# Block-sparse attention and a dropless mixture of experts on one core: the products with V of the third chunk of keys move from the step behind the scores to the step after that

## The chip, the cores and the metric

The kernel runs on one core of one Trainium2 chip, in one launch, on float32 data. The metric is the device time of one execution in microseconds (us), the median of several runs. Next to the runs there is one profiled execution, from which all rows below come.

## The reference

Two blocks follow each other. The first is block-sparse attention (B = 4 batches, H = 8 heads, S = 768 positions, D = 64): each block of 32 queries sees its own block and both neighbours, the first and the last block, and three sampled blocks; the first and the last block of queries see all keys. The second takes the 3072 rows of 512 numbers that come out, sends each to the one of 8 experts with the largest gate logit, and applies that expert's two layers.

```
scores = where(mask, (q @ k.T) / sqrt(D), -1e9)
attn   = exp(scores - max) / (sum(exp) + 1e-9)
x      = concat over heads of (attn @ v)            # (3072, 512)
logits = x @ w_gate                                 # (3072, 8)
e      = argmax(logits);  gate = softmax(logits)[e]
out    = gate * (relu(x @ w1[e]) @ w2[e])           # rows sorted by expert, then put back
```

## The kernel before, in words

**Stages.** In the first 24 us or so the kernel loads q and k of batch 0, turns them, and makes the masks. Then come 48 attention steps up to about 278 us. After that TensorE runs the experts' layers until the end, with weights that were partly loaded during the steps.

**Steps.** The list `steps` (L1321) holds (batch, group, half): a batch has six groups, the group `GL` first and then five regular groups of 128 queries; a half is four heads, that is two pairs `pr`. So steps with an even number are half 0 of a group and those with an odd number half 1. Every step computes the scores of its own half (`scores`, L342, the matmuls at L357), which ScalarE exponentiates (L362) and VectorE masks (L368), and it multiplies the exponentials of the step before by V (`attend`, L392, the matmuls at L386).

**Three chunks of keys.** A regular group's keys come in three chunks of 128: the middle keys together with the ends (chunk 0), and two chunks that end in sampled blocks (chunks 1 and 2). Each of the two tiles `ti` of 64 queries has its own rows of V in chunks 1 and 2. V lies in the tile `around`, which has two parities of five slots: groups use the parities in turn. GpSimd gathers the sampled rows with indirect DMAs from the copy of V in memory; four of them serve one group:

```
def values_of(b, g, ti, ch):                                    # L374
    return around[:, parity(b, g), 2 * ch - 1 + ti if ch else 0, :]
def fetch_values(b, g, ti, ch):                                 # L521; ch 1 here is the third chunk
    nc.gpsimd.indirect_dma_start(
        out=around[p0:, par, 1 + ti + 2 * ch, :], ...
```

In program order GpSimd issues, for the group of steps s and s+1: the gather (ti 0, second chunk) in step s-2, (ti 1, second chunk) and (ti 0, third chunk) in step s-1, and (ti 1, third chunk) at the beginning of step s itself (L1334). Ahead of each stands a one-element copy that reads something of the step (`not_before`, L537): it holds GpSimd's queue until that was written.

**Products.** `attend` runs over chunks, then pairs, heads of a pair and tiles, so a regular step has 24 products, 8 for each chunk. A float32 product is two rows in the trace, so 48 rows. Products 17 to 24 belong to the third chunk; number 18 is the first that reads the gather (ti 1, third chunk).

**Banks.** The products of a step add up in one PSUM bank `op`, taken at the first product (`bank_of`, L377). There are two such banks. `divide` (L441) reads the finished bank on VectorE: it adds a small number to the four sums, takes reciprocals and multiplies, and with half 1 it also starts the DMA of the finished 128 rows to memory (L457). The bank is free for the next user after that.

**Logits.** When both halves of a group are divided, `turn_out` (L464) transposes the rows on TensorE (L469), ScalarE copies them (L471), and `logits` (L484) multiplies them by the gate's weights into spare columns of the bank of the step (L492), from which VectorE copies them (L496). Before the change this happens in every step of half 1, for the group that was finished one step earlier (`out_of`, L1372). When the last group of a batch has its logits, `gate` and, one step later, `gate_weights` follow.

**Order.** The schedule of all five engines is by hand (`manual_schedule`, L283 and L285): each gets its instructions in the order in which the program is written. The order inside a step is: copies that place keys, scores, transposes for the next batch (L178), `turn_out`, products, logits, division, and then the gathers of `fetch_values(*nxt[:2], 0, 0)` in steps of half 0.

Of the kernel before, what the change touches and what calls it, by code (L numbers as in the profile page):

```python
# [17 lines left out]
def kernel(  # L18
# [13 lines left out]
    B, H, S, D = q.shape  # L32
# [7 lines left out]
    E = moe_w_gate.shape[1]  # L40
# [58 lines left out]
    NG = NCH  # L99
    GL = NG - 1  # L100
# [189 lines left out]
    for n in range(2 * NPR):  # L290
        pr, which = n // 2, n % 2
# [97 lines left out]
        )  # L389
        begun.add(ti)  # L390

    def attend(units_):  # L392

        for ch in range(3):
            for b, g, pr, _, e in units_:
                for hh in range(2):
                    for ti in range(2):
                        x = 2 * ch + ti
                        product(b, g, pr, ti, hh, e[:, hh, x * D : (x + 1) * D], values_of(b, g, ti, ch), ch == 2)
# [84 lines left out]
    def logits(b, g, beside=None):  # L484
        xo = xos.pop((b, g))
        if beside is not None:
            lg = banks_of[beside][0][:, 4 * (D + 4) : 4 * (D + 4) + E]
        else:
            lg = ps_o.tile([P, E], F32, name="lgl", tag="op")[:]
        for c in range(DB):  # L490
            for j in range(2):
                nc.tensor.matmul(  # L492
                    lg[j * D : (j + 1) * D, :], lhsT=xo[:, c * P + j * D : c * P + (j + 1) * D], rhs=wg[:, c, :],
                    start=(c == 0), stop=(c == DB - 1), skip_group_check=True,
                )
        nc.vector.tensor_copy(lgn[:, b * NG + g, :], lg)  # L496
# [24 lines left out]
    def fetch_values(b, g, ti, ch):  # L521

        par = parity(b, g)
        t, p0 = tiles_of(g)[ti], 0 if ch else D
        nc.gpsimd.indirect_dma_start(  # L525
            out=around[p0:, par, 1 + ti + 2 * ch, :], out_offset=None, in_=v_d[b][:, :],
            in_offset=bass.IndirectOffsetOnAxis(ap=rows_of[: P - p0, 2 * t + ch : 2 * t + ch + 1], axis=0),
        )
# [8 lines left out]
    def not_before(at):  # L537

        nc.gpsimd.tensor_copy(paced[:], at)
# [779 lines left out]
        fill_stage(b, n // 2, n % 2, n // 2 % 2)  # L1319

    steps = [(b, g, half) for b in range(B) for g in order for half in range(2)]  # L1321
    for i, (b, g, half) in enumerate(steps):
        here = i % (2 * NG)
        prs = (2 * half, 2 * half + 1)
# [2 lines left out]
        if nxt is not None:  # L1327
            b_, g_, half_ = nxt
# [24 lines left out]
        late = here + 2 * NG * (b - B + 2)  # L1353
        for what in PARTS.get(late, ()):
            fetch_part(*what)
        if half == 1 and i + 1 < len(steps):
            not_before(mine[1][4][0:1, 0, 0:1])
            fetch_values(*steps[i + 1][:2], 0, 1)

        copy_turned = None  # L1360
        if b + 1 < B:
            if b == 0 and here < 2:
# [6 lines left out]
        if b + 2 < B and here >= 8:  # L1369
            fill_next(b + 2, here - 8)  # L1370

        out_of = steps[i - 3][:2] if i >= 3 and half == 1 else None  # L1372
        if out_of:
            turn_out(*out_of)
        if copy_turned:
            copy_turned()
        if i > 0 and before[0][1] != GL:
            attend(before)
        elif i > 0:
            for b_, g_, pr, e_all, e in before:  # L1380
                attend_last(b_, pr, e_all, e)
        if "gates" in rt:
            gate_weights()
        if out_of:
            logits(*out_of, beside=steps[i - 1])
            if out_of[1] == order[-1]:
                gate(out_of[0])
        if i > 0:
            divide(*steps[i - 1])
        early(late)  # L1390
        if half == 0 and nxt is not None:
            if i >= 2:
                fetch_ends(*nxt[:2])
                b_, g_, half_ = steps[i - 1]
                not_before(sums[0:1, b_ * NG + g_, 4 * half_ : 4 * half_ + 1])
            fetch_values(*nxt[:2], 0, 0)
        if half == 1 and nxt is not None:
# [8 lines left out]
        if i >= len(steps) - 3:  # L1406
            if i == len(steps) - 1:
                not_before(mine[1][4][0:1, 0, 0:1])
            gather(i - len(steps) + 3)
        before = mine  # L1410
    turn_x(0)
    attend(before)
    divide(*steps[-1])
    attn_by_hand.close()
    fetch(2, 1)
# [171 lines left out]
```

## Time and profile before

| what | us |
|---|---|
| runs, lowest, median, highest | 637.01, 640.93, 645.84 |
| the profiled execution's own time | 638.06 |
| its span, first to last instruction | 636.3 |
| TensorE busy in the span | 608.2 (96%) |
| VectorE, ScalarE, GpSimd busy | 315.6, 231.9, 193.8 |

The span leaves 1.8 us of the execution's time outside. A busy matmul row is not TensorE at its peak: rows overlap, and their ends are modelled. The granted TensorE clock was 0.995 of full speed over the span.

### The profile page before, as it was taken

How to read it: one execution, taken by the hardware profiler on the slowest of the kernel's cores; microseconds unless marked ns; L12 is line 12 of the kernel's file. 1: busy time of each engine (PE TensorE's matmuls, PEld its weight loads, DVE VectorE, ACT ScalarE, POOL GpSimd, SP SyncE). 2: the span in 40 equal slices, each digit the busy share in tenths (PEclk: the TensorE clock that was granted, in tenths of full speed). 3: DMA queues.
4: the chain of work that ended last, by engine and by line, in shares of the span. 5: the costliest groups of instructions: out<-in, count | busy, mean ns of one | idle time of the engine just before them, and what ended most of it. 6: DMA issues, size and time to landing. Idle time of an engine off the chain costs nothing. (4 is left out here: it accounts for less than half of the span.)

```text
span 636.3 us, 20201 instructions
## 1 busy us (share of the span) xinstructions
PE 608.2 (96%) x8326; PEld 516.0 (81%) x8326; DVE 315.6 (50%) x1025; ACT 231.9 (36%) x456; POOL 193.8 (30%) x289
## 2 busy tenths in 40 slices
PE   6899999999999899999999999999999999999994
PEld 6888999998989899997777776877878787967862
DVE  7477767675778567635852485303190118203300
ACT  5376766665667577721111011111112111111110
POOL 2157745643456445720111221011401130020110
PEclk9899999999999999999999999999999999999999
DMA  8899966995696657899999999869998999769710
GB/s 264 207 193 246 288 162 153 255 261 154 136 247 206 184 147 250 261 322 369 338 305 313 344 388 336 303 229 379 396 399 281 365 399 399 291 205 407 299 40 20
DMA packets 125061, 170.86 MB, mean 269 GB/s; under 512 B 71236, under 2 KB 71237, under 8 KB 124934
## 3 DMA queue, kind: packets, MB, share of 16 engines
q1 hardware_dynamic: 114896, 137.61, 66.3%
q0 software_dynamic: 10000, 31.59, 16.0%
q8 instruction: 75, 1.23, 0.8%
q14 instruction: 52, 0.43, 0.2%
q10 hardware_dynamic: 38, 0.00, 0.0%
HBM read 150.11 MB, written 19.33 MB: 266 GB/s over the span
## 5 line engine op out<-in xcount | busy, mean ns | idle before, releaser
L525 POOL DMA_INDIRECT around<-v_rows,rows_of x88 | 100.0, 1136 | 55.3 <-DMA around<-v_rows 21.2
L362 ACT ACTIVATE ea<-s 128x768 f32<-128x768 f32 x104 | 83.6, 811 | 83.2 <-PE s L357 56.1
L1119 DVE STREAM_TRANSPOSE around<-xg 32x128 f32<-32x128 f32 x192 | 58.1, 303 | 86.9 <-DMA xg<-x_rows,gB 81.9
L1138 PEld LDWEIGHTS hp<-around,room 128*128 128x128 f32 x832 | 94.7, 192 | 3.9 <-issue 3.2
L1138 PE MATMUL hp<-around,room 128*128 128x128 f32 x832 | 96.8, 276 | 0.6 <-issue 0.3
L386 PE MATMUL op<-around,ea 128*64 128x65 f32 x2112 | 85.5, 224 | 8.8 <-DMA around<-v_rows,rows_of 5.1
L386 PEld LDWEIGHTS op<-around,ea 128*64 128x64 f32 x2112 | 75.4, 137 | 15.5 <-DMA around<-v_rows,rows_of 6.1
L368 DVE TENSOR_TENSOR ea<-ea,mask 128x768 f32<-128x768 f32 x80 | 74.6, 955 | 14.7 <-ACT ea L362 10.1
L1152 PE MATMUL zp<-room,kr 128*128 128x512 f32 x176 | 77.6, 594 | 0.0
L1145 ACT ACTIVATE kr<-hp 128x512 f32<-128x512 f32 x36 | 21.4, 597 | 116.0 <-PE hp L1138 98.3
L1172 POOL DMA_INDIRECT out_dram<-kr,sB x14 | 14.1, 1008 | 160.2 <-ACT kr L1162 97.9
L1152 PEld LDWEIGHTS zp<-room,kr 128*128 128x128 f32 x176 | 32.6, 190 | 37.2 <-issue 37.2
L357 PE MATMUL s<-other,kr 64*128 64x128 f32 x704 | 48.1, 272 | 0.3 <-issue 0.3
L357 PE MATMUL s<-room,kr 64*128 64x128 f32 x704 | 47.9, 272 | 0.2 <-issue 0.2
L1138 PEld LDWEIGHTS hp<-around,other 128*128 128x128 f32 x384 | 43.8, 192 | 2.3 <-issue 2.3
L1138 PE MATMUL hp<-around,other 128*128 128x128 f32 x384 | 44.3, 275 | 0.0
L357 PEld LDWEIGHTS s<-other,kr 64*128 64x128 f32 x704 | 43.7, 188 | 0.6 <-issue 0.6
L357 PEld LDWEIGHTS s<-room,kr 64*128 64x128 f32 x704 | 43.7, 188 | 0.0
L1250 DVE STREAM_TRANSPOSE ea<-ea 32x128 f32<-32x128 f32 x84 | 21.7, 285 | 30.9 <-DMA ea<-x_rows,gB 30.2
L1162 ACT ACTIVATE kr<-zp,xg 128x512 f32<-128x512 f32 x12 | 8.2, 687 | 74.9 <-PE zp L1152 74.9
L1152 PE MATMUL zp<-other,kr 128*128 128x512 f32 x80 | 35.3, 593 | 0.0
L1119 DVE STREAM_TRANSPOSE around<-kr 32x128 f32<-32x128 f32 x48 | 14.5, 302 | 36.3 <-PE hp L1138 34.9
(369 smaller groups left out, 831.2 us busy)
## 6 DMA issues: line engine op xcount, KB each, us to landing
room<-in_moe_w_dram SPq DMA_DIRECT2D x30, 2048.0 KB
other<-in_moe_w_dram SPq DMA_DIRECT2D x16, 2048.0 KB
room<-in_moe_w_dram SPq DMA_DIRECT2D x16, 512.0 KB
x_rows<-xb SPq DMA_DIRECT2D x20, 256.0 KB
room<-in_k_dram SPq DMA_DIRECT2D x24, 192.0 KB
room<-in_q_dram SPq DMA_DIRECT2D x24, 192.0 KB
v_rows<-room SPq DMA_DIRECT2D x12, 260.0 KB
v_rows<-other SPq DMA_DIRECT2D x12, 260.0 KB
```

The source lines that it names most:

```text
L357: nc.tensor.matmul(s[:, hh, a : a + P], lhsT=keys(r), rhs=moving, start=True, stop=True)
L362: nc.scalar.activation(e, s[:, :, : 6 * D], AF.Exp, scale=scale)
L368: nc.vector.tensor_tensor(e, e, m[:, None, :].to_broadcast([P, 2, 6 * D]), op=ALU.mult)
L386: nc.tensor.matmul(op[ti * D : (ti + 1) * D, pr % 2, hh, : D + 1], lhsT=e, rhs=values[:, (2 * pr + hh) * VW : (2 * pr + hh + 1) * VW], sta ...
L525: nc.gpsimd.indirect_dma_start(out=around[p0:, par, 1 + ti + 2 * ch, :], out_offset=None, in_=v_d[b][:, :], in_offset=bass.IndirectOffsetO ...
L1119: nc.vector.transpose(xT[d, :, t], xg[t, :DM].rearrange("p (c q) -> p c q", c=DB)[:, :, d])
L1138: nc.tensor.matmul(hp[:, m, :], lhsT=st[i]["w1"][:, c, fb * P : (fb + 1) * P], rhs=st[i]["xT"][:, c, :], start=(c == 0), stop=(c == DB - 1),)
L1145: nc.scalar.activation(hT[:, g * (FB // 2) : (g + 1) * (FB // 2), :], hp[:], AF.Relu)
L1152: nc.tensor.matmul(zp[:], lhsT=st[i]["hT"][:, fb, :], rhs=st[i]["w2"][:, fb, :], start=(fb == 0), stop=(fb == FB - 1),)
L1162: nc.scalar.activation(zo, zp[:], AF.Copy, scale=of_i)
L1172: ins = nc.gpsimd.indirect_dma_start(out=to[:, :], out_offset=bass.IndirectOffsetOnAxis(ap=at, axis=0), in_=rows, in_offset=None, bounds_c ...
L1250: nc.vector.transpose(xT_u[d, :, j * P + tq * 32 : j * P + (tq + 1) * 32], xg_u[t, j, :DM].rearrange("p (c q) -> p c q", c=DB)[:, :, d],)
```

## The change

In a regular group the products of the third chunk no longer run in the step behind the scores but in the step after that, ahead of the first two chunks of the next half. A step n counts as split (`in_two`) when its group is regular, it isn't the last step of its batch, and it isn't one of the last four: that is so for 33 of the 48 steps. A split step's bank is closed one step later, so its division, the output rows and the logits of its group go a step later too: `turn_out` and `logits` now stand in steps of half 0 (three steps behind the group's half 1, two for the last group but one; the last group's logits stay behind the steps). In steps with logits these are written beside the closed bank, and this bank is divided behind the logits; in the others the closed bank is divided right behind the third chunk. The gather (ti 0, third chunk) in steps of half 1 is issued behind the third chunk's products, since it overwrites what they read; and the copy that holds back the gather (ti 0, second chunk) in steps of half 0 reads the sums of the bank closed in that step.

```
-    def attend(units_):
-        for ch in range(3):
+    def attend(units_, chunks):
+        for ch in chunks:
...
-            lg = banks_of[beside][0][:, 4 * (D + 4) : 4 * (D + 4) + E]
+            lg = beside[:, 4 * (D + 4) : 4 * (D + 4) + E]
...
+    def in_two(n):
+        return steps[n][1] != GL and n % (2 * NG) != 2 * NG - 1 and n < len(steps) - 4
+    out_at = {}
+    for n in range(1, len(steps) - 2, 2):
+        out_at[n + (3 if n < len(steps) - 4 else 2)] = steps[n][:2]
...
-        if half == 1 and i + 1 < len(steps):
-            not_before(mine[1][4][0:1, 0, 0:1])
-            fetch_values(*steps[i + 1][:2], 0, 1)
...
-        out_of = steps[i - 3][:2] if i >= 3 and half == 1 else None
+        units_of[i] = mine
+        out_of = out_at.get(i)
         if out_of:
             turn_out(*out_of)
...
-        if i > 0 and before[0][1] != GL:
-            attend(before)
...
+        if i > 1 and in_two(i - 2):
+            attend(units_of[i - 2], (2,))
+            closed.append(i - 2)
+            spare = banks_of[steps[i - 2]][0]
+            if not out_of:
+                divide(*steps[i - 2])
+        if half == 1 and i + 1 < len(steps):
+            not_before(mine[1][4][0:1, 0, 0:1])
+            fetch_values(*steps[i + 1][:2], 0, 1)
...
+                attend(units_of[i - 1], (0, 1) if in_two(i - 1) else (0, 1, 2))
+            if not in_two(i - 1):
+                closed.append(i - 1)
...
-            logits(*out_of, beside=steps[i - 1])
+            logits(*out_of, beside=spare)
...
-        if i > 0:
-            divide(*steps[i - 1])
+        for n in closed:
+            if steps[n] in banks_of:
+                divide(*steps[n])
...
-                b_, g_, half_ = steps[i - 1]
+                b_, g_, half_ = steps[closed[0]]
                 not_before(sums[0:1, b_ * NG + g_, 4 * half_ : 4 * half_ + 1])
```

TensorE's order in two consecutive steps of batch 0, a step of half 0 and one of half 1, in the kernel before. `op` with its number is one bank's tile, `s` the scores, `tp` the transposes for the next batch, `xr` those of finished rows; xN counts products or transposes.

```order
L178 MATMUL tp_914<-ident_58,room_75 128x64 x12
L386 MATMUL op_930<-around_78,ea_77 64x65 x24
L357 MATMUL s_995<-room_75,xk_79 128x128 x2
L357 MATMUL s_995<-room_75,kr_80 128x128 x8
L357 MATMUL s_996<-room_75,xk_79 128x128 x2
L357 MATMUL s_996<-room_75,kr_80 128x128 x8
L178 MATMUL tp_1023<-ident_58,room_75 128x64 x12
L469 MATMUL xr_1038<-ident_58,xb_850 128x64 x8
L386 MATMUL op_1050<-around_78,ea_77 64x65 x24
L492 MATMUL op_1050<-wg_63,xo_1047 64x8 x8
```

The same engine in two consecutive steps of the changed kernel, one of half 1 and one of half 0.

```order
L178 MATMUL tp_1008<-ident_58,room_75 128x64 x12
L386 MATMUL op_916<-around_78,ea_77 64x65 x8
L386 MATMUL op_1039<-around_78,ea_77 64x65 x16
L357 MATMUL s_1095<-room_75,xk_79 128x128 x2
L357 MATMUL s_1095<-room_75,kr_80 128x128 x8
L357 MATMUL s_1096<-room_75,xk_79 128x128 x2
L357 MATMUL s_1096<-room_75,kr_80 128x128 x8
L178 MATMUL tp_1121<-ident_58,room_75 128x64 x12
L469 MATMUL xr_1136<-ident_58,xb_945 128x64 x8
L386 MATMUL op_1039<-around_78,ea_77 64x65 x8
L386 MATMUL op_1156<-around_78,ea_77 64x65 x16
L492 MATMUL op_1039<-wg_63,xo_1145 64x8 x8
```

A step still has 24 products, but 8 of them close the bank opened in the step before (`op_1039` has 16 in one step and 8 in the next), and `xr` and the logits stand in the step of half 0.

VectorE's order at the end of a step with logits and the beginning of what follows, in the kernel before. `lgn` are the copied logits, `sums`, `r` and `xb` the three operations of a division, `ea` the exponentials that are masked, `kr` and `xk` placed keys.

```order
L570 COPY kr_80<-room_75 128x4x64
L368 TENSOR_TENSOR ea_77<-ea_77,mask_81 128x768 x2
L496 COPY lgn_64<-op_813 128x8
L445 TENSOR_SCALAR sums_86<-op_813 128x4
L447 RECIPROCAL r_848<-sums_86 128x4
L451 TENSOR_TENSOR xb_850<-op_813,r_848 128x256
L545 COPY around_78<-room_75 64x520
L552 COPY xk_79<-room_75 128x4x64
```

The same in the changed kernel.

```order
L570 COPY kr_80<-room_75 128x4x64
L368 TENSOR_TENSOR ea_77<-ea_77,mask_81 128x768 x2
L496 COPY lgn_64<-op_802 128x8
L445 TENSOR_SCALAR sums_86<-op_802 128x4
L447 RECIPROCAL r_943<-sums_86 128x4
L451 TENSOR_TENSOR xb_945<-op_802,r_943 128x256
L562 TENSOR_LOAD from_k_85
```

The operations of VectorE are the same; logits and division now stand together in the steps of half 0 (no copy to `around` follows there), and `op_802` is the bank that was opened a step earlier than the one that the step's last products go to.

## Rows read from the trace of the kernel before

**Rows 1.** The page's busy time by engine (busy us, share of the span, instructions), and the table by stretch: start and end, length, busy us of each engine with its instructions, granted clock, DMA share and GB/s.

```profile
PE 608.2 (96%) x8326; PEld 516.0 (81%) x8326; DVE 315.6 (50%) x1025; ACT 231.9 (36%) x456; POOL 193.8 (30%) x289
...
45.00:280.00 235.00, 224.48 (x5369) 214.25 (x5367) 160.84 (x484) 154.62 (x309) 127.24 (x196) 1.00 0.80 214
280.00:636.00 356.00, 346.96 (x2276) 267.45 (x2275) 126.62 (x459) 52.78 (x99) 52.25 (x53) 1.00 0.85 311
```

**Rows 2.** Who TensorE waited for from 45 to 280 us: us in total, times, longest.

```profile
PE op L386 <- DMA around<-v_rows,rows_of: 4.7, 6, 1.0
PE s L349 <- issue: 2.6, 5, 0.9
PE op L386 <- issue: 2.3, 6, 0.5
PE s L357 <- issue: 0.3, 1, 0.3
```

**Rows 3.** TensorE in order of time (start, length, engine, line, what, rows merged, and in brackets the idle time before it and what ended it), in two steps of half 1: the first without a stop among its products, the second with one; and the beginnings of the step behind each.

```profile
105.78 1.62 PE L386 MATMUL op<-around,ea 128*64 128x65 f32 x48
107.24 0.59 PE L492 MATMUL op<-wg,xo 128*64 128x8 f32 x16
107.76 0.49 PE L357 MATMUL s<-other,xk 64*128 64x128 f32 x4
...
114.81 0.42 PE L469 MATMUL xr<-ident,xb 64*128 64x64 f32 x8
115.16 1.47 PE L386 MATMUL op<-around,ea 128*64 128x65 f32 x34
117.59 0.62 PE L386 MATMUL op<-around,ea 128*64 128x65 f32 x13 [0.97 <-DMA around<-v_rows,rows_of]
118.62 0.49 PE L357 MATMUL s<-other,xk 64*128 64x128 f32 x4
120.96 0.54 PE L178 MATMUL tp<-ident,room 64*128 64x64 f32 x12
121.42 1.62 PE L386 MATMUL op<-around,ea 128*64 128x65 f32 x48
122.97 0.49 PE L357 MATMUL s<-other,xk 64*128 64x128 f32 x4
```

**Rows 4.** The other places among the products of regular steps at which TensorE stood still for a gather, or for "issue" at the same position; first the whole of one more such step.

```profile
135.92 1.27 PE L386 MATMUL op<-around,ea 128*64 128x65 f32 x34
137.59 0.62 PE L386 MATMUL op<-around,ea 128*64 128x65 f32 x13 [0.41 <-DMA around<-v_rows,rows_of]
138.62 0.49 PE L357 MATMUL s<-other,xk 64*128 64x128 f32 x4
...
54.73 0.62 PE L386 MATMUL op<-around,ea 128*64 128x65 f32 x13 [1.04 <-DMA around<-v_rows,rows_of]
64.79 0.62 PE L386 MATMUL op<-around,ea 128*64 128x65 f32 x13 [0.36 <-issue]
182.66 0.62 PE L386 MATMUL op<-around,ea 128*64 128x65 f32 x13 [0.90 <-DMA around<-v_rows,rows_of]
212.47 0.62 PE L386 MATMUL op<-around,ea 128*64 128x65 f32 x13 [0.73 <-DMA around<-v_rows,rows_of]
274.94 0.62 PE L386 MATMUL op<-around,ea 128*64 128x65 f32 x13 [0.67 <-DMA around<-v_rows,rows_of]
```

**Rows 5.** GpSimd in order of time from 106 to 119 us: the gathers, in the order (ti 1, second chunk), (ti 0, third chunk), (ti 1, third chunk) of the group whose products of half 0 start at 115.16, then one (ti 0, second chunk) and so on for the next group.

```profile
106.24 0.94 POOL L525 DMA_INDIRECT around<-v_rows,rows_of  x1 [0.16 <-issue]
108.21 0.98 POOL L525 DMA_INDIRECT around<-v_rows,rows_of  x1 [0.54 <-PE op L492]
110.52 1.70 POOL L525 DMA_INDIRECT around<-v_rows,rows_of  x1 [0.48 <-issue]
112.68 0.18 POOL L539 COPY paced<-sums 1x1 f32<-1x1 f32 x1 [0.46 <-DVE sums L445]
113.40 0.94 POOL L525 DMA_INDIRECT around<-v_rows,rows_of  x1 [0.54 <-issue]
```

**Rows 6.** VectorE in order of time in the same steps: the two masks of the step, then logits and division.

```profile
114.69 1.97 DVE L368 TENSOR_TENSOR ea<-ea,mask 128x768 f32<-128x768 f32 x2
119.19 0.17 DVE L496 COPY lgn<-op 128x8 f32<-128x8 f32 x1 [2.53 <-PE op L492]
119.28 0.15 DVE L445 TENSOR_SCALAR sums<-op 128x4 f32<-128x4 f32 x1
119.46 0.18 DVE L447 RECIPROCAL r<-sums 128x4 f32<-128x4 f32 x1
119.67 0.42 DVE L451 TENSOR_TENSOR xb<-op,r 128x256 f32<-128x256 f32 x1
```

**Rows 7.** TensorE at the stops among products of steps of half 0.

```profile
176.09 1.30 PE L386 MATMUL op<-around,ea 128*64 128x65 f32 x26 [0.34 <-issue]
197.81 0.71 PE L386 MATMUL op<-around,ea 128*64 128x65 f32 x17 [0.49 <-issue]
241.18 1.13 PE L386 MATMUL op<-around,ea 128*64 128x65 f32 x30 [0.35 <-issue]
250.68 1.01 PE L386 MATMUL op<-around,ea 128*64 128x65 f32 x26 [0.34 <-issue]
260.13 0.99 PE L386 MATMUL op<-around,ea 128*64 128x65 f32 x26 [0.36 <-issue]
```

More of the change, by code (lines that the diff above doesn't have):

```diff
@@ L1321 @@
     steps = [(b, g, half) for b in range(B) for g in order for half in range(2)]
+    units_of = {}
+    def in_two(n):
[3 more added lines that the diff above has]
+        out_at[n + (3 if n < len(steps) - 4 else 2)] = steps[n][:2]
     for i, (b, g, half) in enumerate(steps):
@@ L1376 @@
             copy_turned()
-        if i > 0 and before[0][1] != GL:
-            attend(before)
-        elif i > 0:
-            for b_, g_, pr, e_all, e in before:
-                attend_last(b_, pr, e_all, e)
+        closed = []
+        spare = None
+        if i > 1 and in_two(i - 2):
[7 more added lines that the diff above has]
+            fetch_values(*steps[i + 1][:2], 0, 1)
+        if i > 0:
+            if steps[i - 1][1] == GL:
+                for b_, g_, pr, e_all, e in units_of[i - 1]:
+                    attend_last(b_, pr, e_all, e)
+            else:
+                attend(units_of[i - 1], (0, 1) if in_two(i - 1) else (0, 1, 2))
+            if not in_two(i - 1):
+                closed.append(i - 1)
+                spare = spare if spare is not None else banks_of[steps[i - 1]][0]
         if "gates" in rt:
@@ L1409 @@
             gather(i - len(steps) + 3)
-        before = mine
     turn_x(0)
-    attend(before)
+    attend(units_of[i], range(3))
     divide(*steps[-1])
```

## The prediction

> **What bounds the kernel now.** I read the busy time by engine first, then the table by stretch, then who TensorE waited for, and last the order of time on TensorE, GpSimd and VectorE around those waits. In the first [rows 1] the reader sees TensorE busy for 608.2 of 636.3 us, so all its idle time is 28.1 us, and no order of the work can win more than that unless busy time shrinks. The table by stretch puts 235 − 224.5 = 10.5 us of it in the steps from 45 to 280 us, where the change acts, and 9 us into the experts' stretch, which has little more than its end. VectorE (160.8 of 235), ScalarE (154.6) and GpSimd (127.2) have room. So the steps are bound by TensorE, and the change can pay only through TensorE's stops.
>
> The list of TensorE's waits [rows 2] names them: 4.7 us for gathered rows of V, six times, never over 1.0; 2.6 us at the scores of group GL; 2.3 us of "issue" among the products. The order of time [rows 3, 4] shows where a gather stops it: each time behind 34 rows of a step of half 1, that is behind 17 products, in front of number 18. That is the first that reads (ti 1, third chunk), the gather issued last, in the step in which the scores are made. The "issue" of 0.36 us at 64.79 sits at the same place and I count it as the same wait. The change gives exactly this read one more step.
>
> **What a stop costs.** The idle time is less than the loss, because rows overlap. A step without a stop goes from its first product to the next scores in 107.76 − 105.78 = 1.98 us; with a stop of 0.97 it takes 118.62 − 115.16 = 3.46 [rows 3]. The loss is 1.48, so 0.51 more than is shown idle. At 135.92 it is 138.62 − 135.92 − 1.98 = 0.72 for an idle 0.41 [rows 4], so 0.31 more. The Trainium skill, Perfetto Trace Analysis, section Identifying the Most-Contended Engine, says that busy time of matmuls is no good measure of headroom, since they are pipelined; the trace agrees, with 1.48 us lost where 0.97 is idle. By idle time alone the gain would be 4.4 us.
>
> **The sum.** Six stops lie in steps that the change touches: 0.97 [rows 3], 0.41, 1.04, 0.36, 0.90 and 0.73 [rows 4], together 4.41 us. With 0.51 for the first and 0.31 for each of the other five the loss is 4.41 + 0.51 + 1.55 = 6.5 us. The stop of 0.67 at 274.94 [rows 4] stays: its half is one of the last four, which aren't split.
>
> **Is the gather in time a step later?** The gather for the stop at 117.59 begins at 110.52 and leaves GpSimd at 112.22 [rows 5]; TensorE goes on at 117.59, so the rows landed about 5.4 us behind. Without the stop TensorE would have wanted them at 115.16 + 1.47 = 116.6. In the changed order product 18's work comes ahead of the other products of the next step, where products now start at 121.42 [rows 3], less the 1.5 us that the stop cost: 119.9. So there are 119.9 − 112.2 = 7.7 us for a landing of 5.4.
>
> **What is late next.** The second chunk's gather (ti 1) leaves GpSimd at 106.24 + 0.94 = 107.2 [rows 5]. It is read behind 16 of the 24 products in the changed step (8 of the old half, then the first chunk), and `turn_out`, 0.34 us (115.16 − 114.81) [rows 3], no longer stands ahead: about 115.16 − 0.34 + 16 × (1.46 ÷ 24) = 115.8, with 107.24 − 105.78 = 1.46 for 24 products. That leaves 8.6 us for 5.4. The moved gather (ti 0, third chunk) waits for the third chunk's products of the same step, but already waits for the step's last mask: the masks end at 116.66 [rows 6], and those products would end near 115.16 − 0.34 + 0.5 = 115.3 [rows 3], so nothing is added. The gather that goes by the sums now waits for logits first in steps of half 0: 0.52 us of logits, `turn_out` 0.34 and a copy of 0.17 [rows 3, 6] make about 1 us, against 13 us from its issue at 113.40 [rows 5] to its read three steps on. I cost all three at nothing; the cover is the margin of 3 us or more, and if it went, a stop like those above would come back.
>
> **The banks.** There are two, and now each is open over two steps. A bank closed in a step with logits must be divided before the first two chunks of the next step begin. From the end of logits to the end of the division goes 120.09 − 118.62 = 1.5 us [rows 3, 6]. TensorE meanwhile has scores and transposes (121.42 − 118.62 = 2.8) and 8 products (0.5) [rows 3], 3.3 us in all. The margin is 1.8 us, so I cost it at nothing. Products, transposes and logits stay the same in number. No row shows a step's products go from one bank to the other: the dearest reading is the 0.09 us by which 24 products take longer ahead of scores (1.55, from 121.42 to 122.97) than ahead of logits (1.46) [rows 3], 33 × 0.09 = 3 us; the other end is the stops in steps of half 0 [rows 7], 1.88 us idle and 3.4 with 0.31 more for each, which fall away if they are waits after all. I take zero, since products within one run follow each other without a gap.
>
> Output rows and their logits go out one step later. The first routing of tokens now follows the gate in the same step; VectorE has 74 us idle over 235 [rows 1], and TensorE waits for none of it. SyncE's queue gets the output rows later, behind the same neighbours; I cost that at nothing.
>
> So the profiled execution, whose time is its span and 1.8 us around it, goes from 638.06 to 631.6. The median of the runs is 640.93, 2.9 us above it. If that difference is more of the same stops it goes too; if not it stays. I take half of it, and so predict 633.0.
>
> **Rivals.** (a) The gain is half: TensorE runs ahead by what it wins, the bus stays as busy (DMA share 0.80 [rows 1]), and gathers of the second chunk, or the banks, stop it instead in some steps. For it: TensorE and gathers follow each other closely. Against: no stop before product 17 in any half 1 of this trace. 638.06 − 3.2 + 2.9 = 637.7.
>
> (b) The stop isn't the gather's landing at all, so the order changes nothing: 640.9. What speaks for it is that 5.4 us is long for a gather. Against: the stops stand at one product in all seven cases [rows 3, 4], and only half 1, which reads the rows first, has them. The Trainium skill, DMA: Bandwidth & Descriptors, section Anatomy of one DMA — SWDGE (gpsimd) path, gives about 2.0 us plus bytes ÷ 436e3; for 128 rows of 520 floats I estimate 2.6 us by that page, and by it no gather here would have been late. The trace's 5.4 us is the measured one, on a bus that others share.
>
> (c) Slower: in steps with logits the division behind them frees the bank too late, and the first product into it waits in the next step. It decides when VectorE's division ends more than 3.3 us behind the logits, where 1.5 is seen. At 2.6 us of extra lateness each of some 18 such steps would lose 0.8 us, 14 us in all: 638.06 − 6.5 + 14.4 = 646. For it: VectorE also has masks and key copies in that order. Against: the masks end at 116.66 and VectorE then sat idle for 2.53 us before the logits [rows 6].
>
> (d) More: the stops of half 0 [rows 7] were waits too and go as well: 631.6 − 3.4 = 628.2. Against: these stand behind 17 to 31 rows, not at one product, and half 1 of a group reads rows that half 0 has read before.
>
> **How the numbers follow.** I give the forecast 0.54, (a) 0.20, (b) 0.06, (c) 0.09, (d) 0.11. The forecast's own range is 630 to 636, from the unknown costs above and the 2.9 us between execution and median. The range over cases goes from 627.0, which leaves out the better part of (d), to 642.0, which leaves out most of (c): some 15 in 100 outside. A measurement of this kernel can tell about 2% from no change, 12.8 us. Faster by over 2% is below 628.1: half of (d), 0.06 rounded up. Slower is above 653.7: the worst of (c), 0.03. The rest, 0.91, is within.
>
> **What would show it.** In the changed kernel TensorE's waits for gathers should fall from six to at most one or two, none behind the first chunk's products; products of a split step should take 1.5 us from first to next operation, in two banks; busy time of TensorE from 45 us to the end of the steps should stay near 224 us, and the steps should end about 6 us sooner, with the experts' stretch as long as before. It is wrong if stops appear at the first product into the second bank (banks), behind 16 products of a step (second chunk), or if the same six losses stand in front of the third chunk a step later; and if the steps end sooner but the experts' stretch grows by as much.

## The result and the profile after

The changed kernel takes 645.17 us (median of 20 runs, 641.57 to 654.45) where the kernel before takes 640.35 (20 runs on the same chip): a ratio of 1.0081, 95% interval 1.0059 to 1.0103. Forecast were 633.0 and a gain of 6.5 us; what came is a loss of 4.8 us, outside the range. Two repeats, the second on a faster chip, gave 1.0069 (1.0042 to 1.0095) and 1.0074 (1.0041 to 1.0106): the loss is small and steady.

The profiled execution took 641.82 us with a span of 640.1, against 638.06 and 636.3 before. Busy time and the table by stretch, to be held against [rows 1] (the last stretch here ends with the span):

```profile
PE 614.4 (96%) x8326; PEld 521.6 (81%) x8326; DVE 316.6 (49%) x1025; ACT 231.4 (36%) x456; POOL 201.6 (31%) x289
...
45.00:280.00 235.00, 222.63 (x5308) 211.92 (x5304) 159.29 (x474) 152.50 (x305) 131.08 (x194) 0.99 0.79 209
280.00:640.10 360.10, 350.48 (x2337) 270.57 (x2335) 127.85 (x463) 53.45 (x100) 54.19 (x55) 1.00 0.85 309
```

TensorE is busy for 222.6 of 235 us where it was 224.5: its idle time has grown by 1.9 us in the very stretch in which 4.4 should have gone. Who it waited for from 45 to 280 us, against [rows 2]:

```profile
PE op L386 <- issue: 3.3, 10, 1.1
PE tp L178 <- DMA room<-in_k_dram: 1.6, 1, 1.6
PE s L349 <- issue: 1.3, 3, 0.5
PE op L492 <- ACT xo L471: 1.0, 4, 0.3
...
PE tp L178 <- ACT ea L362: 0.8, 1, 0.8
PE op L386 <- DMA around<-v_rows,rows_of: 0.8, 1, 0.8
```

This is the first reading to make. The waits for gathered rows went from six (4.7 us) to one (0.8), and that one stands in the halves that are not split. So the mechanism of the change works. But three kinds of wait are new: loads of K, the copy of the rows for the logits (`xo`), and ScalarE's exponentials in front of transposes. The waits called "issue", which have no named releaser, grew from 2.3 to 3.3 us among the products (1.1 of it is one stop in step 46) and fell from 2.6 to 1.3 us in the scores of group GL.

A pair of split steps in order of time, against [rows 3] and [rows 4]: a step of half 1 and the step of half 0 with logits behind it.

```profile
112.84 0.49 PE L357 MATMUL s<-other,xk 64*128 64x128 f32 x4
...
115.64 1.62 PE L386 MATMUL op<-around,ea 128*64 128x65 f32 x48
117.19 0.49 PE L357 MATMUL s<-other,xk 64*128 64x128 f32 x4
...
120.43 1.68 PE L386 MATMUL op<-around,ea 128*64 128x65 f32 x48
...
122.58 0.49 PE L357 MATMUL s<-other,xk 64*128 64x128 f32 x4
```

24 products in two banks take 117.19 − 115.64 = 1.55 us, as before in one: the change of bank costs nothing. The pair takes 4.35 + 5.39 = 9.74 us, where the pair that ends in the stop of [rows 3] took 118.62 − 107.76 = 10.86. So where a stop goes and nothing takes its place, a pair wins a microsecond.

Where then does the time go? Three marks divide the steps in both traces. Step 5 begins (its scores) at 49.37 before and 47.84 after, step 45 at 261.44 and 260.60, and the experts' first transposes, in the kernel before, at

```profile
275.96 0.66 PE L1127 MATMUL tp<-ident,xg 128*128 128x128 f32 x4
```

and at 279.60 after. So steps 5 to 44 take 212.07 us before and 212.76 after, although the gathers' stops are gone (in a second pair of profiles on another chip it is 210.01 and 213.29, so one profile is good to some 2 us here); the last three take 14.52 and 19.00, of which 8 products that have moved into them explain 0.5. The experts' stretch is as long as before (360.3 and 360.5 us from that mark to the end). One loss is an expected gain that never came, the other is 4 us at the end of the steps.

The second is plain to see, in TensorE, ScalarE and GpSimd in order of time in step 46:

```profile
266.22 0.49 PE L357 MATMUL s<-other,xk 64*128 64x128 f32 x4
...
269.34 0.38 PE L469 MATMUL xr<-ident,xb 64*128 64x64 f32 x5 [0.31 <-issue]
...
271.55 2.13 PE L386 MATMUL op<-around,ea 128*64 128x65 f32 x42 [1.07 <-issue]
...
270.14 0.81 ACT L362 ACTIVATE ea<-s 128x768 f32<-128x768 f32 x1 [4.60 <-PE xr L469]
...
265.81 0.98 POOL L525 DMA_INDIRECT around<-v_rows,rows_of  x1 [0.55 <-issue]
267.10 0.95 POOL L1056 DMA_INDIRECT xg<-x_rows,gA  x1 [0.30 <-issue]
268.36 0.95 POOL L525 DMA_INDIRECT around<-v_rows,rows_of  x1 [0.30 <-issue]
269.61 0.95 POOL L1056 DMA_INDIRECT xg<-x_rows,gA  x1 [0.30 <-issue]
```

The step takes 8.26 us, from 266.22 to 274.48, where 4.01 was the time before (without logits, which add 0.9). TensorE trickles and ScalarE begins its first exponential 2.5 us late, both without a releaser that fits. Behind it the granted clock falls, to 0.57 over 4 us, most of it at the lower of its two levels, 1.2 GHz; before that stretch TensorE had been busy for 2.23 of 4 us. The table by stretch, with columns as in [rows 1] (the granted clock is the last but two):

```profile
268.00:272.00 4.00, 2.23 (x42) 1.84 (x40) 0.96 (x1) 1.08 (x2) 1.95 (x3) 1.00 0.83 319
272.00:276.00 4.00, 4.00 (x70) 3.98 (x67) 1.79 (x5) 1.02 (x2) 0.00 (x0) 0.57 0.51 198
```

These two losses are what the experiments take apart.

### The profile page after: what moved, and what is told of

Read it like the earlier page. It is cut to its first block, busy times and chain, and to the rows that moved or that the text cites. A ratio compares the mean times of both kernels' runs of the same rounds, so it can differ in the third digit from the quotient of the medians.

```text
span 640.1 us, 20199 instructions
## 1 busy us (share of the span) xinstructions
PE 614.4 (96%) x8326; PEld 521.6 (81%) x8326; DVE 316.6 (49%) x1025; ACT 231.4 (36%) x456; POOL 201.6 (31%) x289
## 5 line engine op out<-in xcount | busy, mean ns | idle before, releaser
L525 POOL DMA_INDIRECT around<-v_rows,rows_of x88 | 102.5, 1165 | 53.8 <-DMA around<-v_rows 22.0
L386 PE MATMUL op<-around,ea 128*64 128x65 f32 x2112 | 83.6, 225 | 5.1 <-issue 3.3
```

The source lines that it names most:

```text
L386: nc.tensor.matmul(op[ti * D : (ti + 1) * D, pr % 2, hh, : D + 1], lhsT=e, rhs=values[:, (2 * pr + hh) * VW : (2 * pr + hh + 1) * VW], sta ...
L525: nc.gpsimd.indirect_dma_start(out=around[p0:, par, 1 + ti + 2 * ch, :], out_offset=None, in_=v_d[b][:, :], in_offset=bass.IndirectOffsetO ...
```

## The experiments

The runs come in five groups: that of part 1, that of part 2, two of part 3, and that of part 4. Each group has its own chip and runs of the kernel before on it. The chips are not alike: the kernel before took 639.9 and 638.6 us in the first two groups (and 640.35 with the result above), and 630.1, 628.4 and 629.0 in the last three. So ratios are compared, and traces, where it can be done, with traces of the same kind of chip.

**1. The two halves of the change, each alone.** The changed kernel once more, with nothing edited, and the kernel before:

> The changed kernel once more, for a second profile. Time about 645 us, ratio to the kernel before 1.006 to 1.010. Theory A (the logits moved to the steps of half 0 cost time there): steps of half 0 that have logits and transposes take 5.3 to 5.5 us again, where 5.1 would be their sum, TensorE waits for the copied rows xo in several of them, and the stop of 4 us in the last but one step need not come back. Theory B (the end of the steps): the last but one step takes over 8 us again, where 4.0 is its sum, and the granted clock falls behind it.

> The kernel before once more, for a second profile: 635 to 647 us; four to seven stops for gathers behind 34 rows, each 0.4 to 1.0 us; steps of half 0 of 4.35 us where there is no stop, and no step near 8 us among the last four.

Logits and rows out moved to half 0, no product split:

```diff
 def in_two(n):
-    return steps[n][1] != GL and n % (2 * NG) != 2 * NG - 1 and n < len(steps) - 4
+    return False
```

> No step is split: the third chunk stays where it was before, but output rows are turned and logits made in steps of half 0, as in the changed kernel. Theory A: slower than before by 5 to 10 us (645 to 650), since it has the cost and not the gain; the stops for gathers behind 34 rows come back, four to seven of them. Theory B, if the third chunk or its gather is what makes the end late: as before, 640.

Products split, logits kept in half 1 (a step later again):

```diff
-    out_at[n + (3 if n < len(steps) - 4 else 2)] = steps[n][:2]
+    late_by = {1: 3, 2 * NG - 3: 3, 2 * NG - 1: 2}.get(n % (2 * NG), 4)
+    out_at[n + (late_by if n < len(steps) - 5 else 3 if n == len(steps) - 5 else 2)] = steps[n][:2]
```

> Steps are split as in the changed kernel, but the rows of most groups are turned and their logits made one step later still, in steps of half 1 as before (for the group GL and the ones at a batch's end in steps of half 0). Theory A: the gain of some 6 us comes out: 633 to 636. Theory B, or a cost in the split itself: 643 to 647, like the changed kernel.

Measured, as ratios to the kernel before: 1.0069 (1.0042 to 1.0095) for the repeat, 1.0023 (0.9991 to 1.0055) for the logits alone, 1.0035 (1.0014 to 1.0056) for the split alone. Step 46 took 8.84 us in the repeat, 7.84 with the split alone, 5.74 with the logits alone, 4.07 in the kernel before. The split alone costs a little, the logits alone can't be told from no change, neither pays, and the split alone has no wait at all for gathered rows from 45 to 280 us.

**2. The stop in step 46.** First the last six halves left whole, so that steps 44 to 47 issue what they issue before; then the same with the split alone; then SyncE's two loads of step 46 moved to 47; then the gathers of x one step later:

```diff
-    return steps[n][1] != GL and n % (2 * NG) != 2 * NG - 1 and n < len(steps) - 4
+    return steps[n][1] != GL and n % (2 * NG) != 2 * NG - 1 and n < len(steps) - 6
...
-    out_at[n + (3 if n < len(steps) - 4 else 2)] = steps[n][:2]
+    out_at[n + (3 if n < len(steps) - 6 else 2)] = steps[n][:2]
```

> The changed kernel, but the last six halves (instead of four) stay whole and the logits of the last three groups stay where the kernel before has them, so that steps 44 to 47 issue what they issue before. The changed kernel's step 46 takes 8.3 to 8.8 us from scores to scores where about 4.9 is its work, and the clock is halved for 3.4 us behind it. Theory B (that stop is most of the loss): step 46 is back at 4.0 to 4.3 us, the granted clock stays at full there, and the time is 3 to 4 us under the changed kernel, 640.3 to 641.5, within 0.2% of the kernel before. Theory A (the loss is spread over the steps of half 0 with logits, through ScalarE): the time stays within 1 us of the changed kernel, 643.5 to 645, and the steps before 42 are as in the changed kernel. Rival C (the stop belongs to whatever step comes last but one, or follows the last split step): a stop of 3 us or more shows up in step 44 to 47 all the same.

> The split of the products alone, with logits in steps of half 1, and with the last steps as in the kernel before. With the end of the changed kernel it took 641.4 us, 1.5 over the kernel before, of which the stop in step 46 (7.8 us where 4.9 is its work) was about 3. Theory B: it takes 638 to 638.7 us, 0.2 to 0.3% faster than the kernel before, since the split wins about 1.5 us in a batch's regular stretch and pays some of it back at the batch's start. If the split wins nothing even so (the stops at gathers had cover, the prediction's rival b), it takes 640 us or more. The prediction's own sum would have it at 633 to 635, since all six stops are gone.

```diff
-    PARTS |= ... | {n: [(1, 1, 2 * n - 44), (1, 1, 2 * n - 43)] for n in (22, 23)}
+    PARTS |= ... | {23: [(1, 1, part) for part in range(4)]}
```

> The changed kernel with the two quarter loads of expert 1's first weights that SyncE issues in step 46 moved behind, to step 47, where two others stand already. In the changed kernel SyncE issues them at 267.1 us, behind output rows that it waited for, and TensorE and ScalarE stop between 268.6 and 271.6. If these 512 KB on the queues are the cause of the stop, step 46 falls from 8.3 us to about 5, with no half clock behind it. If they are not, step 46 stays at 7.5 to 9 us.

```diff
-        if i >= len(steps) - 3:
+        if i >= len(steps) - 2:
             if i == len(steps) - 1:
+                gather(1)
                 not_before(mine[1][4][0:1, 0, 0:1])
-            gather(i - len(steps) + 3)
+            gather(2 * (i - len(steps) + 2))
```

> The changed kernel with the gathers of rows of x for experts 0 and 1 one step later each (46 and 47 instead of 45 and 46). GpSimd issues them at 267.1 and 269.6 us in the changed kernel, around the stop in step 46. If they are its cause, step 46 falls from 8.3 us to about 5; the transposes of expert 0's rows behind step 47 may then wait a little. If they are not, step 46 stays at 7.5 to 9 us.

In none of the four did step 46 come back to its work: it took 6.74, 6.78, 7.20 and 7.40 us (the last two are one run each). The first is telling: its steps 45 to 47 issue what the kernel before issues, and 2.7 us are lost in step 46 all the same; the ratio stayed at 1.0068 (1.0040 to 1.0096). The split alone with plain end came out at 0.9995 (0.9956 to 1.0034), where 0.997 or 0.998 was expected. TensorE in that kernel, step 46, products:

```profile
266.80 1.26 PE L386 MATMUL op<-around,ea 128*64 128x65 f32 x22
268.43 0.35 PE L386 MATMUL op<-around,ea 128*64 128x65 f32 x5 [0.36 <-issue]
269.16 0.38 PE L386 MATMUL op<-around,ea 128*64 128x65 f32 x5 [0.38 <-issue]
...
270.65 0.57 PE L386 MATMUL op<-around,ea 128*64 128x65 f32 x11 [0.37 <-issue]
```

No product here waits for a semaphore, and still they come in spurts of 5 rows, 0.74 us apart. So the order of the last steps and the weight loads are excluded. The gathers of x are not: in the last run they stand one step later in the program, but GpSimd, which was ahead, started them at 268.58 and 269.83 us, still in step 46 (267.10 and 269.61 in the changed kernel). What all of these share with the changed kernel is that GpSimd's last gathers follow each other without a pause; that gave theory C.

**3. Theory C: gathers in a row.** The gathers of x held back behind masks, on the split alone with plain end and on the changed kernel:

```diff
-        if i >= len(steps) - 3:
-            if i == len(steps) - 1:
-                not_before(mine[1][4][0:1, 0, 0:1])
-            gather(i - len(steps) + 3)
+        if i >= len(steps) - 2:
+            not_before(mine[half][4][0:1, 0, 0:1])
+            for row in range(half, 2 * half + 1):
+                gather(row)
```

> Split of the products alone, plain end, and the gathers of rows of x for experts 0 and 1 held back: the first until the first mask of step 46, the second (with the third) until the last mask of step 47. Theory C: it is GpSimd's gathers, issued one behind the other, that stop the issue of TensorE and ScalarE. In every kernel with a long step 46 three or four gathers start within 2.6 to 4.3 us of each other and the stop begins 0.6 us behind the start of the third; in the kernel before masks on VectorE held the second and third back (1.71 and 1.40 us instead of 0.95) and nothing stopped. By C step 46 falls from 6.8 us to 4.0 to 4.6, and the time from 638.5 to 635.5 to 636.5, which is 0.3 to 0.5% under the kernel before. If something else stops step 46, it stays at 6 us or more and the time at 638 to 639. A wait of up to 1 us in front of expert 0's transposes may take a part away.

> The changed kernel and nothing else than that holding back of the gathers for experts 0 and 1. Theory C: step 46 falls from 8.3 to 8.8 us to about 5, the half clock behind it is gone, and the time goes from 644 to 640 to 641. If the stop isn't the gathers', 643 to 645.

The first of these with one more gather moved, out of the rows of group GL:

```diff
+            if g == GL and i > 2:
+                fetch_values(*steps[i + 1][:2], 0, 0)
...
+                if g != GL:
                     not_before(sums[0:1, b_ * NG + g_, 4 * half_ : 4 * half_ + 1])
-            fetch_values(*nxt[:2], 0, 0)
+            if g != GL or i < 2:
+                fetch_values(*nxt[:2], 0, 0)
```

> As the split alone with held-back gathers, and in the second step of each batch but the first, the gather that started 1.1 to 1.5 us into the 96 rows of group GL's scores goes behind that step's mask. Over ten profiles those rows take 1.56 us where no gather starts between 0.6 us ahead of them and 1.25 us into them, and 2.4 to 2.9 us where one does. Theory C: in steps 13 and 25 they fall from 2.7 to 2.8 us to 1.56, in step 37 they stay near 1.6, and the time is 2 to 3 us under its sister without this edit, 633 to 634. If rows of GL are slow for another reason (clock, banks), they stay at 2.7 us and the times are the same. If the later gather is read too early, a stop of TensorE for it shows up two steps on.

And the kernel before with three gathers put in a row at four places:

```diff
             fetch_values(*steps[i + 1][:2], 0, 1)
+            if i in (17, 19, 29, 31):
+                fetch_values(*steps[i + 1][:2], 1, 0)
+                fetch_values(*steps[i + 1][:2], 1, 1)
```

> The kernel before; only in steps 17, 19, 29 and 31 the three gathers that otherwise go apart (by waits for keys, mask and keys) follow each other behind the mask of that step. Theory C: TensorE stops for 0.4 us or more without a named releaser in most of these four steps or the ones behind them, beginning about 0.6 us behind the start of the third gather, 3 us or more in all over the same steps of the kernel before when the stops for gathered rows are set aside. If the row of gathers is harmless, such stops stay at the 0 to 0.4 us that these steps show in the kernel before.

Step 46 fell to 3.99, 4.64 and 3.98 us, as C had it. But the times did not follow: 1.0028 (0.9992 to 1.0064), 1.0099 (1.0064 to 1.0134) and 0.9950 (0.9916 to 0.9984); and the crowded kernel had two unnamed stops (0.51 and 0.45 us), both at rows of GL, none near its rows of gathers. This chip was of the faster kind, so kernels with and without the holding back were run side by side on one more chip:

> The changed kernel once more, on one chip with its paced sister. Theory C (gathers issued in a row stop TensorE and ScalarE): step 46 takes 8 us or more here while the sister's takes 5 or less. If the chip decides it, both are long or both are short.

> The changed kernel with the gathers for experts 0 and 1 held back. Theory C: step 46 at about 5 us, and 2 to 4 us less time than the changed kernel on the same chip. If only the chip decided: step 46 as long as its sister's, and the same time.

> The split alone, logits in half 1, plain end, gathers as they were. On one chip it was 0.9995 of the kernel before with step 46 at 6.8 us. Theory C: 0.997 to 1.003, step 46 at 6 us or more.

> The same with the last gathers held back and one gather of each batch's second step behind its mask: 0.995 of the kernel before on one chip (interval 0.992 to 0.998). Theory C: 0.992 to 0.998 again, 2 to 4 us under its unpaced sister, step 46 at about 4 us, and rows of GL in steps 13 and 25 at 1.6 to 2.2 us. If that was the chip's doing, it is the same as its sister.

Ratios: 1.0074 (1.0041 to 1.0106), 1.0141 (1.0095 to 1.0187), 1.0056 (1.0021 to 1.0091) and 1.0024 (0.9996 to 1.0052). The changed kernel on this chip, nothing held back, GpSimd and then TensorE in step 46:

```profile
266.01 0.98 POOL L525 DMA_INDIRECT around<-v_rows,rows_of  x1 [0.54 <-issue]
267.30 0.95 POOL L1056 DMA_INDIRECT xg<-x_rows,gA  x1 [0.30 <-issue]
268.55 0.95 POOL L525 DMA_INDIRECT around<-v_rows,rows_of  x1 [0.30 <-issue]
269.81 0.95 POOL L1056 DMA_INDIRECT xg<-x_rows,gA  x1 [0.30 <-issue]
...
265.26 0.49 PE L357 MATMUL s<-other,xk 64*128 64x128 f32 x4
...
269.90 0.49 PE L357 MATMUL s<-other,xk 64*128 64x128 f32 x4
```

The same four gathers, 1.25 us apart, and the step takes 4.64 us without a stop. Gathers in a row are not enough for the stop: it comes and goes with the chip. Whether they are needed for it stays open, since no kernel with held-back gathers ran on a chip of the first kind. And holding them back makes the changed kernel slower (by about 4 us on this chip): TensorE then waits 2.8 us for rows of V in step 45, and 2.6 us for expert 1's rows of x behind the steps, where it waited for none. So the times with held-back gathers say little about theory C. That the version with 0.9950 beats the kernel before did not hold on a second chip.

What is left is the more useful fact: the changed kernel loses 0.7% here too, without the stop. Its waits from 45 to 262 us on this chip:

```profile
PE tp L178 <- DMA room<-in_k_dram: 4.6, 3, 2.5
PE s L357 <- issue: 1.7, 2, 0.9
```

**4. Theory D: the gate holds SyncE's queue.** The transposes of K for the next batch read loads that SyncE issues two steps ahead. Here is SyncE from step 26 on, in the kernel before (first trace):

```profile
167.13 0.37 SPq L517 DMA_DIRECT2D x_rows<-gw  x1
...
170.85 3.21 SPq L161 DMA_DIRECT2D other<-in_v_dram  x4
174.16 1.80 SPq L140 DMA_DIRECT2D room<-in_k_dram  x2
```

and in the changed kernel (the run on the faster chip), with TensorE at step 30's transposes:

```profile
171.46 1.17 SPq L161 DMA_DIRECT2D other<-in_v_dram  x2
175.72 0.37 SPq L517 DMA_DIRECT2D x_rows<-gw  x1
...
178.92 2.97 SPq L140 DMA_DIRECT2D room<-in_k_dram  x2
...
187.26 0.59 PE L178 MATMUL tp<-ident,room 64*128 64x64 f32 x12 [2.48 <-DMA room<-in_k_dram]
```

The four writes of gate weights (`gate_weights`, L517 and L519) need the logits of the batch's last group, and these come a step later now. So the writes stand behind two of the four loads of V shown, instead of ahead of all four; SyncE's queue, which goes in order, stands still from 172.63 to 175.72, and the K load behind it starts late. TensorE's stop in step 30 is in all three traces of kernels with the late gate on the faster chips (2.27, 2.35 and 2.48 us).

In the first trace of the changed kernel the writes are as late: they begin at 173.30 and the K load at 176.48, where the kernel before issued it at 174.16 for a step that came 2.6 us later. But there the load doesn't stop TensorE. The stop at step 30's transposes is short and ended with an exponential of ScalarE:

```profile
184.40 0.59 PE L178 MATMUL tp<-ident,room 64*128 64x64 f32 x12 [0.84 <-ACT ea L362]
```

Of the other five traces with the late gate on the first chips one has a stop for K there, of 1.26 us.

Taking the late writes alone away:

```diff
+        def write():
+            nc.sync.dma_start(x_d[first : first + GL * P, DM:].rearrange("(c p) w -> p c w", p=P), gw[:, :GL])
+            for p, n, row in pieces(GL):
+                nc.sync.dma_start(x_d[b * S + row : b * S + row + n, DM:], gw[p : p + n, GL, :])
...
+            later.append(write)
...
+        while writes:
+            writes.pop(0)()
         units_of[i] = mine
...
-            gate_weights()
+            gate_weights(writes)
```

The loop over `writes` stands in the next step, behind its load of K and so behind the loads of V of the step before.

> The changed kernel, but SyncE's four writes of gate weights go behind the loads of V and K of the next step instead of ahead of them. In the changed kernel SyncE waits for the gate until 173.3 us and issues step 30's K load at 176.5 us (174.2 in the kernel before, whose step 30 comes 2.6 us later). Theory D (the later gate holds SyncE's queue, and the K load behind it stops TensorE): the K load comes 2 us or more earlier against its step, the stop in step 30 goes, and the time is 1.003 to 1.005 of the kernel before instead of 1.007 to 1.008. Rival E (loads are bound by the bus, whatever stands ahead of them in the queue): waits for K stay at 1.5 to 4.6 us in steps 45 to 262 us of the trace, and the ratio stays at 1.006 to 1.009. The stop of step 8 (1.5 us), ahead of which no gate is written, stays in both.

> The kernel before once more, for its trace on the same chip. By the traces so far TensorE waits 3 to 6 us for gathered rows between 45 and 262 us, not at all for K, and step 46 takes 4.0 us.

Measured: 0.9992 (0.9969 to 1.0015). No loss can be told, which is more than D expected. SyncE and the same transposes in this kernel:

```profile
173.56 1.43 SPq L140 DMA_DIRECT2D room<-in_k_dram  x2
175.09 0.65 SPq L519 DMA_DIRECT2D x_rows<-gw  x1
...
183.10 0.54 PE L178 MATMUL tp<-ident,room 64*128 64x64 f32 x12
```

The load has 183.10 − 173.56 = 9.5 us and TensorE doesn't wait; step 30 takes 5.02 us instead of 7.72. Rival E, that the bus sets the loads whatever the order, is out for this stop. It holds in part for step 8, where no gate is written: there a wait of 0.8 us is left.

But the stop is a part of the loss only: 2.7 us of step 30, where the fall of the ratio is worth some 5 us. The split alone, whose gate is not late, has its K load in time on the very chip on which the changed kernel has that stop:

```profile
169.89 1.51 SPq L140 DMA_DIRECT2D room<-in_k_dram  x2
...
178.62 0.54 PE L178 MATMUL tp<-ident,room 64*128 64x64 f32 x12
```

Its ratio there was 1.0056 (1.0021 to 1.0091) all the same, where the changed kernel's was 1.0074. So on that chip the late gate is not needed for a loss. The mended kernel was not run beside the changed one, and what else lies between 1.007 and 0.999 no run shows.

The mended kernel's waits from 45 to 262 us:

```profile
PE s L357 <- issue: 4.5, 4, 2.3
PE op L386 <- DMA around<-v_rows,rows_of: 1.5, 1, 1.5
PE s L349 <- issue: 1.4, 1, 1.4
PE tp L178 <- DMA room<-in_k_dram: 0.8, 1, 0.8
```

and the longest of the kernel before on the same chip, up to 275 us:

```profile
PE op L386 <- DMA around<-v_rows,rows_of: 6.0, 8, 1.5
```

So with the queue mended one of the gathers' eight stops is left (1.5 of 6.0 us, in a half that isn't split), and other stops stand in their place. From 45 us to the end of the steps all stops together come to 9.7 us in the mended kernel, to 12.3 in the changed one of part 3 and to 6.6 in the kernel before. By these traces the mended kernel would still be slower than the one before; its profiled execution took 630.32 us, over its median of 628.70, and that of the kernel before 626.09, under its median of 628.95. So they show that new stops use up the gain, and not why the medians are equal.

## Why the prediction was wrong

**The gathers.** Right. Six stops fell to one, in the halves that stay whole, as said; no stop behind 16 products of a step, none at a new bank, 1.55 us for a step's products. Rivals (b) and (c) are out; that the 646 of (c) lies near the 645.17 measured is chance, since no product waited for a bank.

**The step that failed** is that the 6.5 us were taken as won, and all that TensorE runs into in the gathers' place was costed at nothing. "The steps should end about 6 us sooner"; on the chip of the result they ended 279.60 − 275.96 = 3.6 us later. Steps 5 to 44 took as long as before, with new stops at transposes (1.6 and 0.8 us) and logits (1.0 us), and step 46 took 8.26 us instead of 4.01. What stops step 46 is open.

One of these zeros has a cause that an edit shows, on the faster chips: "SyncE's queue gets the output rows later, behind the same neighbours; I cost that at nothing." Output rows are not all that hangs on the logits. The gate of a batch does too, and its four writes go through the same queue, ahead of loads of K that TensorE wants two steps on. The prediction said that "the first routing of tokens now follows the gate in the same step", looked at VectorE for it, and never looked at SyncE's order. Moving the writes took step 30 from 7.72 to 5.02 us. The ratio went from 1.007 to 0.999, some 5 us, but on different chips, and the rest of that is not placed. On the chip of the result TensorE did not stop for the late load.

**What is late next.** The prediction asked this of gathers and banks only. TensorE arrives at step 8 at 62.30 instead of 65.81 and wants its K 3.3 us sooner; SyncE issues the load at 56.70 instead of 57.47, 0.8 us sooner. The difference is the new stop there:

```profile
66.41 0.59 PE L178 MATMUL tp<-ident,room 64*128 64x64 f32 x12 [1.60 <-DMA room<-in_k_dram]
```

Loads that had 10.7 us before (57.47 to 68.15) have 8.1 now, and take 9.7. This is rival (a), which had the right idea (TensorE runs ahead into the next transfer) with half the price and the wrong transfers: it named the second chunk and the banks. In the mended kernel nothing of the gain is left, so the price is all of it, not half; how much of that is transfers isn't shown, since the largest part of its stops (4.5 us, in front of scores) has no named releaser.

**The logits in half 0** were given no cost. On the first chip their step takes 5.39 us where the kernel before has 5.02 for the same work in half 1, and TensorE waits 1.0 us in four places for `xo`; on the faster kind of chip it is 5.02 again. Alone, this part gave 1.0023 with no effect in its interval.

**The stop in step 46** nobody forecast. It cost 2.3 to 4 us in seven traces of six kernels on the first chips and 0.8 with the logits alone, nothing in the kernel before, and is absent on the others, where the loss is as large. It is settled that the order of the last steps and the weight loads don't decide it; what does is open. So is what sums to the loss on the first chips, since the mended kernel was not run there.

**The sum.** The 6.5 us of gain were 4.8 us of loss by the medians, and with the queue mended, on another chip, 0.25 us of gain (628.70 against 628.95), which is inside the noise.

## What to carry to other kernels

When a result is delayed by a step, list everything that hangs on it down to the last DMA, and look in each in-order queue at what stands behind: the wait of a small write is paid by the big load that follows. And when a stop is removed, price the next transfer that the engine will run into, in every queue that feeds it, by its issue time and its lead in the trace; a load need not come sooner because the engine does (at step 8 TensorE came 3.3 us sooner and the load's issue 0.8). Set a doubtful pair of kernels side by side on more than one chip before a stop of one trace is called the cause, and a mended kernel beside the one that it mends.

## What the runs showed of the hardware

A gather that GpSimd starts while a mask runs on VectorE is held until the mask is over. In the kernel before, GpSimd and VectorE:

```profile
268.63 1.71 POOL L1056 DMA_INDIRECT xg<-x_rows,gA  x1 [0.30 <-issue]
...
268.56 0.96 DVE L368 TENSOR_TENSOR ea<-ea,mask 128x768 f32<-128x768 f32 x1 [1.25 <-ACT ea L362]
```

It ends at 270.34, 0.82 us behind the mask's end, where a gather alone takes 0.95. One that starts just ahead of a mask isn't held (267.30 above, 0.95, with a mask from 267.54). The Trainium skill, GPSIMD Engine Reference, section Specifications, says that GpSimd's access to SBUF is shared with VectorE and contends with instructions that have two SBUF inputs, as the mask has; the trace agrees.

On the first chips dense work on TensorE is slower where a gather starts in it. The 96 rows of GL's scores (L349) take 1.56 us at their shortest. In the kernel before at step 12 one starts at 84.85 and they take 2.62, with a stop as its 0.98 us end:

```profile
84.47 1.27 PE L349 MATMUL s<-other 64*64 64x64 f32 x46
86.15 1.01 PE L349 MATMUL s<-other 64*64 64x64 f32 x50 [0.40 <-issue]
```

On the faster kind of chip the same collision (a gather 0.27 us into the rows) gives 1.92 us and no stop. In the ten traces of the first kind all 31 such phases from step 12 on with a gather in their first 1.25 us took 2.0 to 3.1 us. Of the 29 others 18 took 1.56 to 1.60 us, but 11 took 2.1 to 3.8. So a gather goes with the slow rows, and it is not their only cause: "1.56 us where no gather starts", as an expectation above has it, is too simple. Why the chips differ, no run here tells.
